# One ring of three shared PSUM pairs for attention scores, and x transposed by DMA

## The chip, the core and the metric

One core of one Trainium2 chip. The metric is the device time in us of one execution, taken on the chip; lower is better. Profiles are single executions; their span (first to last instruction) is some 1.8 us shorter than the same execution's device time. The kernel before takes 811.6 us (median; 811.2 to 812.7).

The names used below: PE is the matmul engine; ACT (ScalarE) and DVE (VectorE) work on vectors; SP serves here to issue transfers (DMA), and ACT's queue issues some too. PE writes its results to banks of PSUM, and two banks make a "pair". A "pass" is the scores of two heads in one pair, a "fill" is PE writing a pass, a "visit" is a run of fills with no other PE work between. PV is the product of the exponentiated scores with V; mish is the activation of branch B. The "head" of the span lasts until the first exp, the "tail" begins when the last exp has ended, and the "stretch" lies between.

## The reference

Input x is 2048 x 640 (bf16). Two branches read it, and a gate mixes them:

```python
g = sigmoid((x * gate_w).sum(-1, keepdims=True))
# A: 32 heads of 20 columns, full softmax attention over 2048 keys, then wo (640 x 640)
scores = einsum("bhqd,bhkd->bhqk", q, k) * 20 ** -0.5
a = (softmax(scores) @ v) @ wo
# B: dense 640 -> 1536, mish, dense 1536 -> 640
h = x @ w1 + b1
b = (h * tanh(softplus(h))) @ w2
out = g * a + (1 - g) * b
```

The exps of the scores are the bulk of the work: 32 heads x 2048 x 2048.

## The kernel before

The kernel does not run in the order of its text. Every piece of work is a task with an engine, an estimated cost and its needs; a planner (`Order.run`) walks through a model of the engines at build time and emits the tasks in the order in which the model starts them. The order on each engine is therefore fixed before the launch, and any change of a cost, a need or a constant may give a wholly different order.

Heads are taken in groups `G` of four heads by 512 queries (32 groups). For each group and each of 16 blocks of 128 keys, the scores of four heads are made in two passes, each with two PE matmuls into a pair of PSUM banks. Most key blocks are exponentiated by ACT (one ACTIVATE of 128x1024 for a pass). `SHARE[G]` of the 16 blocks go to DVE, which builds a bit-level approximation in three terms (per block two L779 for the first, a half each, and two L793 for the others). A "PV" matmul group then adds the result to the output of the head.

```python
SHARE = (3, 3, 4, 5, 4, 6, ...)          # key blocks for DVE by group, 143 in all
...
R = {k: Ring(...) for k, n in (
    ("S0", 1), ("S1", 1), ("X", 1), ("D", 1), ("E", (13, 6, 48)), ...)}   # PSUM: S0, S1, D pairs; X, C single banks
...
ld_x = {0: [load_x((nc.scalar, nc.sync)[s % 2], s, s + 1, ...) for s in range(4)]}
ld_w0 = [load((nc.sync, nc.scalar)[t], w0[:, t], ...) for t in range(2)]   # weights of the first four heads
ld_x[1] = [load_x(nc.sync, 4, 8, 6500)]
ld_wv = load(nc.sync, wv, ...)
ld_x[2] = [load_x(nc.scalar, 8, 12, 9000)]
ld_x[3] = [load_x(nc.sync, 12, 16, 11000)]
ld_gw = load(nc.sync, gw[:, :, 0:1], ...)
ld_wqk = load(nc.sync, wqk[:, :, 0:2 * D], ...)
...
for s in range(4):                        # chunk 0 of x: PE transposes, then a copy; tile 1 by ACT
    ...
    (nc.scalar.copy if s == 1 else nc.vector.tensor_copy)(out=xt[:, 0, :, s * P:(s + 1) * P], ...)
for c in range(1, 4):                     # chunks 1 to 3: PE transposes, copies by DVE
    ...
for n, blk in enumerate(passes):          # passes for ACT: two buffers by turns
    sb, eb = Buf(R["S%d" % (n % 2)]), Buf(R["E"])
    ...
    nc.scalar.activation(eb.tile[:, 0:w * QC], sb.tile[:, 0:w * QC], ACT.Exp, scale=inv)
...
xb = Buf(R["D"])                          # passes for DVE: a buffer of their own
```

The softmax here doesn't subtract the row's maximum and nothing guards it: scores larger than these inputs give would overflow.

## Time and profile before

| | before |
|---|---|
| device time, median | 811.6 us |
| first exp starts | 10.3 us |
| stretch from the first exp to the end of the last | 781.6 us, 738 exps |
| tail after it | 19.3 us |

Which lines carry this, and how they are read, is in the prediction. Two more views of the kernel before are needed later. First, what the queues waited for (engine and line, what it waited for, us, times, longest; a q behind an engine's name is its sequencer, which also issues DMAs):

```profile
SPq L423 <- DVE xt L472: 1.6, 1, 1.6
SPq L423 <- DMA arena<-in_A_x_dram: 1.2, 1, 1.2
```

L423 is the line that issues a load. An issue that waits for an earlier transfer to land (the second line: wv's issue at 3.83 us waited for an x tile that landed at 3.81) is a thing to note. Second, the chain of waits up to the first exp (start, length, what):

```profile
1.65 7.26 DMA wvt<-in_A_wqkv_dram
...
8.95 0.46 PE S L557 x20
9.42 0.49 PE D L557 x12
9.90 0.42 PE S L716 x4
10.33 1.92 ACT es L744 x2
```

The first exp hangs on the landing of the first weights at 8.9 us; ACT's own queue does not appear after 1.6 us.

### The profile page before, as it was taken

The numbers are of one execution on the slowest core, as the hardware profiler recorded it, in microseconds if no ns is written. First come the engines' busy times: TensorE is split into PE (matmuls) and PEld (weight loads), VectorE is DVE, ScalarE is ACT, GpSimd is POOL, SyncE is SP. The second block draws the span as 40 slices with busy tenths as digits, with TensorE's granted clock in tenths as the row PEclk, the third lists the DMA queues.
The fourth block names the chain that finished last, engine by engine and source line by source line (L and its number), as shares of the span: only waits on it lengthen the run. The fifth ranks groups of instructions, "written<-read, shape, count | busy, mean of one in ns | idle before, by whom it ended". The sixth has DMA issues, their size and how long they took to land.

```text
span 811.1 us, 24412 instructions
## 1 busy us (share of the span) xinstructions
PE 776.3 (96%) x10642; PEld 281.7 (35%) x10642; DVE 706.3 (87%) x949; ACT 774.0 (95%) x791; POOL 6.6 (1%) x10
## 2 busy tenths in 40 slices
PE   8999999999999989999999998999999989999998
PEld 4432333333333333333332334333332333333336
DVE  3788899998888899999999998889999989978994
ACT  5899999999999999999999999999999999999991
POOL 3000000000000000000000000000000000000000
PEclk9999999999999999999999999999999999999999
DMA  9601100000000000000000000000000000001112
GB/s 314 186 16 24 19 16 7 19 19 16 18 8 19 19 15 6 19 20 20 20 19 15 22 4 19 16 19 19 20 7 19 19 19 4 20 19 32 32 40 76
DMA packets 32273, 25.21 MB, mean 31 GB/s; under 512 B 17762, under 2 KB 26914, under 8 KB 32166
## 3 DMA queue, kind: packets, MB, share of 16 engines
q1 hardware_dynamic: 30694, 22.55, 9.9%
q8 instruction: 83, 1.36, 0.7%
q10 hardware_dynamic: 1472, 1.10, 0.4%
q14 instruction: 24, 0.20, 0.1%
HBM read 18.20 MB, written 2.88 MB: 26 GB/s over the span
## 4 chain that ended last, share of the span: by engine, by line
PE 58%; ACT 33%; DVE 4%; issue 4%; DMA 1%; ACTq 0%; DVEq 0%
ACT es L744 23%; PE S L716 19%; PE C L703 17%; PE X L517 11%; ACT arena L933 7%; PE X L577 3%; PE X L557 3%; DVE t L779 2%; PE X L597 1%; ACT bs L744 1%; PE D L517 1%; DMA wvt<-in_A_wqkv_dram 1%; PE D L716 1%; ACT L933 1%; PE C L399 1%
## 5 line engine op out<-in xcount | busy, mean ns | idle before, releaser
L744 ACT ACTIVATE es<-S 128x1024 bf16<-128x1024 f32 x708 | 666.5, 1033 | 13.2 <-PE C L703 4.6
L779 DVE TENSOR_SCALAR t<-D 128x1024 uint16<-128x1024 f32 x286 | 349.2, 1221 | 52.1 <-PE D L716 48.5
L716 PE MATMUL S<-q,kt 32*128 32x512 bf16 x1476 | 285.9, 384 | 15.7 <-ACT es L744 12.1
L793 DVE TENSOR_SCALAR t<-t 128x2048 uint16<-128x2048 uint16 x286 | 190.2, 681 | 1.3
L716 PEld LDWEIGHTS <-kt 32*128 32x128 bf16 x2048 | 80.5, 91 | 273.7 <-issue 263.5
L703 PE MATMUL C<-es,va 128*32 128x512 bf16 x1416 | 140.6, 385 | 1.3 <-DVE oraw L826 1.2
L716 PE MATMUL D<-q,kt 32*128 32x512 bf16 x572 | 111.3, 385 | 4.1 <-DVE t L779 3.5
L703 PE MATMUL C<-t,vs 128*32 128x512 bf16 x1144 | 106.3, 383 | 0.3 <-DVE t L793 0.2
L517 PE MATMUL X<-w,arena 128*32 128x320 bf16 x1536 | 82.0, 305 | 0.1
L703 PEld LDWEIGHTS <-va 128*32 128x32 bf16 x2048 | 54.5, 95 | 79.3 <-issue 65.1
L517 PE MATMUL X<-xt,w 128*32 128x512 bf16 x960 | 72.3, 383 | 2.5 <-DVE arena L919 1.4
L933 ACT ACTIVATE arena<-arena 128x2048 bf16<-128x2048 bf16 x36 | 68.0, 1911 | 0.3
L703 PE MATMUL C<-t,va 128*32 128x512 bf16 x572 | 58.0, 383 | 1.7 <-DVE t L779 1.7
L517 PEld LDWEIGHTS <-arena 128*32 128x32 bf16 x1536 | 33.4, 96 | 33.5 <-issue 26.4
L557 PE MATMUL X<-xt,wqk 128*32 128x512 bf16 x560 | 44.2, 383 | 0.0
L577 PE MATMUL X<-xt,wqk 128*32 128x512 bf16 x560 | 43.8, 383 | 0.0
L919 DVE TENSOR_SCALAR arena<-X,b 128x512 bf16<-128x512 f32 x48 | 35.7, 745 | 4.8 <-PE X L517 4.5
L703 PEld LDWEIGHTS <-vs 128*32 128x32 bf16 x1144 | 29.9, 95 | 28.3 <-issue 20.5
L517 PEld LDWEIGHTS <-w 128*32 128x32 bf16 x960 | 22.7, 95 | 30.6 <-issue 22.7
L744 ACT ACTIVATE bs<-S 128x1024 bf16<-128x1024 f32 x30 | 29.7, 1031 | 0.8 <-PE S L716 0.6
L597 PE MATMUL X<-wvt,xt 128*128 128x160 bf16 x310 | 28.3, 234 | 1.9 <-DVE va L602 0.9
L399 PE MATMUL C<-xt,gw 128*32 128x512 bf16 (+4 forms) x396 | 28.1, 359 | 0.0
(92 smaller groups left out, 362.0 us busy)
## 6 DMA issues: line engine op xcount, KB each, us to landing
rbc<-rows SPq DMA_DIRECT2D x124, 64.0 KB
w<-in_B_w_dram SPq DMA_DIRECT2D x2, 1920.0 KB
out_dram<-arena SPq DMA_DIRECT2D x16, 160.0 KB
oc<-on SPq DMA_DIRECT2D x96, 20.0 KB
wqk<-in_A_wqkv_dram SPq DMA_DIRECT2D x1, 1600.0 KB
arena<-in_A_x_dram SPq DMA_DIRECT2D x2, 640.0 KB
wvt<-in_A_wqkv_dram SPq DMA_DIRECT2D x1, 800.0 KB
arena<-in_A_x_dram ACTq DMA_DIRECT2D x1, 640.0 KB
```

The lines of the kernel that those rows point to most:

```text
L399: nc.tensor.matmul(t[32 * r:32 * r + 32, 0:n], lhsT=gw[:, 0, 1:33], rhs=xt[:, r, 0, 0:n], start=G is None, stop=G is None, tile_position=( ...
L517: nc.tensor.matmul(t[32 * r:32 * r + 32, 0:width], lhsT=lhsT(r), rhs=rhs, start=a, stop=b, tile_position=(0, 32 * r))
L557: nc.tensor.matmul(t[32 * r:32 * r + 32, 0:n], lhsT=w, rhs=xt[:, sc, k, lo:hi], start=k == 0, stop=k == KT - 1, tile_position=(0, 32 * r))
L577: nc.tensor.matmul(t[32 * r:32 * r + 32, 0:QC], lhsT=w, rhs=xt[:, qc, k, :], start=k == 0, stop=k == KT - 1, tile_position=(0, 32 * r))
L597: nc.tensor.matmul(t[:, n * 160:(n + 1) * 160], lhsT=xt[:, js[n] // 4, k, (js[n] % 4) * P:(js[n] % 4 + 1) * P], rhs=wv[:, k, 160 * b:160 * ...
L703: nc.tensor.matmul(acc[G][32 * r:32 * r + 32, :], lhsT=vs4[:, b, term - 1, DVE_KEYS.index(j), h:h + 32] if term else va4[:, b, j, h:h + 32 ...
L716: nc.tensor.matmul(t[:, off * QC:(off + 1) * QC], lhsT=kt[32 * r:32 * r + 32, (p % 2) * S + j * P:(p % 2) * S + (j + 1) * P], rhs=q_buf[G] ...
L744: nc.scalar.activation(eb.tile[:, 0:w * QC], sb.tile[:, 0:w * QC], ACT.Exp, scale=inv)
L779: nc.vector.tensor_scalar(out=bufs[0].tile[:, 2 * QC * hp:2 * QC * (hp + 1)], in0=xb.tile, scalar1=P * LOG2E * inv, scalar2=P * (127 - log ...
L793: (nc.vector if eng == "DVE" else nc.gpsimd).tensor_scalar(out=bufs[i].tile[:, a * w:(a + 1) * w], in0=bufs[0].tile[:, a * w:(a + 1) * w], ...
L919: lambda t: nc.vector.tensor_scalar(out=hs[:, ft, :], in0=t[:, 0:QC], scalar1=b1[:, ft:ft + 1], scalar2=None, op0=ALU.add),
L933: nc.scalar.activation(v, hs[:, 4 * a:4 * a + 4, :] if i == 0 else v, func, bias=1.0 if i == 1 else 0.0)
```

## The change

Its intent: any of three pairs serves ACT or DVE, so that a score pass need not wait for its own fixed buffer; two ACT passes may be filled in one visit of PE where two pairs are free; the planner's latencies are corrected; chunks 1 to 3 of x are transposed on their way in by DMA, which frees PE and DVE at the start; and all constants are searched anew for the planner. The core of the diff (cut: the other constants, the planner's latencies, single-line cost changes, the deterministic order of the last four small steps):

```diff
-SHARE = (3, 3, 4, 5, 4, 6, ...)      # 143 key blocks to DVE
+SHARE = (2, 3, 4, 5, 5, 5, ...)      # 133
...
-        ("S0", 1), ("S1", 1), ("X", 1), ("D", 1), ("E", (13, 6, 48)), ...
+        ("S", 3), ("X", 1), ("E", (17, 6, 56)), ...
...
-        sb, eb = Buf(R["S%d" % (n % 2)]), Buf(R["E"])
+        sb, eb = Buf(R["S"]), Buf(R["E"])
...
-            xb = Buf(R["D"])
+            xb = Buf(R["S"])
...
+        if S and S[1].before2:           # pick_pe: wait for two free pairs, or until it is late for one
+            ...
+                free = S[1].rings[0].ring.free
+                if len(free) > 1:
+                    end = free[1][0]
+                last = 0 if self.mode == "row" else (S[1].before.end or ...) - self.EARLY
+                S = max(S[0], min(end + self.LAT["ACT"], last)), S[1]
...
-    ld_x = {0: [...]}; ld_w0 = [load((nc.sync, nc.scalar)[t], ...)]; ld_x[1] ... ld_wv, ld_gw, ld_wqk by nc.sync
+    ld_x = [load((nc.scalar, nc.sync)[t % 2], xs[:, t, :], ...) for t in range(NU)]     # chunk 0 alone
+    for c in range(1, NQ):
+        for k in range(KT):
+            t_xt[c, k] = o.add("SP", 5000, lambda c=c, k=k: nc.sync.dma_start_transpose(
+                out=xt[:, c, k, :], in_=x2d[c * QC:(c + 1) * QC, k * P:(k + 1) * P]), prio=0)
+    ld_w0 = [load(nc.scalar, w0[:, t], ...) for t in range(2)]
+    ld_wv = load(nc.scalar, wv, ...)
+    ld_gw = load(nc.scalar, gw[:, :, 0:1], ...)
+    ld_wqk = load(nc.scalar, wqk[:, :, 0:2 * D], ...)
...
-    for c in range(1, 4):                # PE transposes and DVE copies of chunks 1 to 3
-        ...
```

## The prediction

> **What bounds the kernel now.** I first read the page's share of busy time and the 40 slices, then the groups of instructions, then one table by stage, and last the start times of the exps one by one.
>
> ```profile
> PE 776.3 (96%) x10642; PEld 281.7 (35%) x10642; DVE 706.3 (87%) x949; ACT 774.0 (95%) x791; POOL 6.6 (1%) x10
> ...
> L744 ACT ACTIVATE es<-S 128x1024 bf16<-128x1024 f32 x708 | 666.5, 1033 | 13.2 <-PE C L703 4.6
> L779 DVE TENSOR_SCALAR t<-D 128x1024 uint16<-128x1024 f32 x286 | 349.2, 1221 | 52.1 <-PE D L716 48.5
> L716 PE MATMUL S<-q,kt 32*128 32x512 bf16 x1476 | 285.9, 384 | 15.7 <-ACT es L744 12.1
> L793 DVE TENSOR_SCALAR t<-t 128x2048 uint16<-128x2048 uint16 x286 | 190.2, 681 | 1.3
> ...
> L399 PE MATMUL C<-xt,gw 128*32 128x512 bf16 (+4 forms) x396 | 28.1, 359 | 0.0
> ```
>
> PE and ACT are both near full, but PE's share contains 28.1 us of matmuls that only keep its clock up (L399), so PE has some room. ACT has none: its work is 738 exps (708 to es, 30 to bs) and 36 mish passes. The stage table says where ACT is not busy (columns: stretch, its length, PE, PEld, DVE, ACT, POOL, clock, DMA share, GB/s):
>
> ```profile
> 0.00:10.30 10.30, 7.48 (x90) 3.65 (x94) 2.54 (x13) 2.56 (x3) 6.11 (x8) 1.00 0.82 251
> 10.30:50.00 39.70, 36.36 (x440) 16.42 (x438) 28.39 (x52) 35.23 (x38) 0.00 (x0) 1.00 0.58 191
> 50.00:400.00 350.00, 338.32 (x4504) 117.51 (x4500) 312.85 (x417) 346.84 (x354) 0.51 (x2) 1.00 0.07 17
> 400.00:791.90 391.90, 378.81 (x5228) 132.38 (x5223) 353.55 (x456) 386.56 (x394) 0.00 (x0) 1.00 0.07 19
> 791.90:811.00 19.10, 15.32 (x400) 11.77 (x393) 8.96 (x13) 2.77 (x5) 0.00 (x0) 0.96 0.23 80
> ```
>
> So the span is a head of 10.3 us (until the first exp), an ACT stretch of 781.6, and a tail of 19.2. In the stretch ACT looks idle for only 13 us. That hides most of the loss, because exps overlap: one lasts 1.03 us, but in the timeline the next can start 0.90 after it.
>
> ```profile
> 67.62 1.02 ACT L744 ACTIVATE bs<-S 128x1024 bf16<-128x1024 f32 x1
> 68.52 1.03 ACT L744 ACTIVATE es<-S 128x1024 bf16<-128x1024 f32 x1
> 69.42 1.05 ACT L744 ACTIVATE bs<-S 128x1024 bf16<-128x1024 f32 x1
> ```
>
> I took the start-to-start time of all 723 exps that follow an exp: 349 at about 904 ns, 181 at about 920, and a long tail up to 4.4 us. Together 689.8 us, mean 954. 723 x 0.904 = 653.6, so 36.2 us are lost to late scores, not 13. The other 91.8 us of the stretch (781.6 - 689.8) are mish, table loads and steps into and out of them. Setting each exp beside its fill gives the cause: in the groups that come late by under 0.4 us, the exp starts 486 ns after its last score matmul, and that matmul came late because PE was in other work when the pair became free. One example:
>
> ```profile
> 351.39 0.40 PE L703 MATMUL C<-t,vs 128*32 128x512 bf16 x4
> 351.54 1.22 DVE L779 TENSOR_SCALAR t<-D 128x1024 uint16<-128x1024 f32 x1 [0.75 <-PE D L716]
> 351.62 0.72 PE L517 MATMUL X<-w,arena 128*32 128x320 bf16 x16
> 352.27 0.39 PE L716 MATMUL S<-q,kt 32*128 32x512 bf16 x2
> 352.59 0.32 PE L517 MATMUL X<-w,arena 128*32 128x320 bf16 x4
> 352.76 1.94 ACT L744 ACTIVATE es<-S 128x1024 bf16<-128x1024 f32 x2 [0.18 <-PE S L716]
> ```
>
> The exp at 352.76 follows its fill (352.27) by 0.49; sixteen dense matmuls stood ahead of it. The idle column says 0.18, the start-to-start loss is 0.30. With two pairs (S0, S1) a fill must start within some 0.29 us of the end of the exp two before it (1.81 - 1.03 - 0.49), and one PE group with its switch uses that up.
>
> **What the Trainium skill says.** "ScalarE: Activation LUTs", What ACT_TABLE_LOAD costs: an ACTIVATE with immediates takes 186 ns + 0.833 N (1039 for N = 1024) and back-to-back ones overlap by about 93 ns. The trace agrees on the length (1033) and shows a larger overlap, about 0.13. "TensorEngine Tiling (Array Packing)", Key Properties: changing the tiling mode drains PE. The trace agrees: a score pass comes 312 ns after the last column group and the next column group 318 after it, where two column groups stand 216 apart; a visit thus costs 318 + 312 - 216 = 414 ns net, and a visit with two pairs (325) 421. "Perfetto Trace Analysis", Identifying the Most-Contended Engine: repeating gaps on the engine that should be full can mean too few PSUM buffers; that is the pattern here. "DMA: Bandwidth & Descriptors", DMA Transpose (X-bar): bf16 may be transposed on its way into SBUF, from SP or ACT alone; the kernel before has no such transfer, so no trace confirms its speed yet.
>
> **The change part by part.** *Shares.* The DVE list sums to 133 keys in place of 143. A key is two exps on ACT or two L779 and two L793 on DVE. ACT gets 20 more exps (758): 20 x 0.904 = +18.1 us, wholly on the bound. DVE loses 20 x (1.221 + 0.681) = 38.0. PE loses 20 PV groups of 0.216 (three terms become one), 4.3 us.
>
> *Ring.* S0, S1 and D become three pairs that any score pass may take. Passes stay 1024 in all (738 + 286 before, 758 + 266 after). Before, 735 visits held them, 275 of them with two. If the scheduler now gets some 620 visits, PE saves 115 x 0.41 = 47 us, which is slack for being on time, not time off the end. The size of the gain is the part of the 36.2 us that goes. By class: the 181 at 920 ns (2.9 us) stay, since their fills are not late. The 185 between 930 and 1300 (26.2 us) are the late fills; I keep a quarter, 6.5. A single fill into a third free pair would have 0.9 us more room; but two S pairs filled in one visit come when only one full pair is left, so their slack is again about 0.29 us, and DVE still holds a pair for the 1.22 us of L779. Hence a quarter and not zero. The 7 above 1300 (7.4 us) include 3.5 us at 30.6 where ACT waited for a PV (exp buffers full); the exp ring grows from 13 to 17 slots, so I keep 3.0. Sum left: 12.4.
>
> *DMA transposes.* Gone are 60 PE transposes (4.7 us at an estimated 78 ns, from eight in 0.62) and nine evictions (6 x 0.69 + 3 x 0.42 = 5.4 us of DVE), all beside exps in the first 31 us. New are 15 transfers of 128 KB on SP. In the head, DMA is 82% busy, and the first K product waited 0.84 us for its weights. Those weights now move to ACT's queue ahead of wv, which should help; but all remaining weight loads are issued from ACT before its first copy. On SP the last two of them, gw and wqk, took 1.97 and 2.51 us to issue; on ACT they would hold up the copy that Q needs. I net this at +0.5, between -1 and +4. Tail: the pairs of the last product rotate over three buffers, but PE is busy for 15.3 of 19.1 us there, so -0.5.
>
> Sum of the span: head 10.3 + exps (723 + 20) x 0.904 = 671.7 + other ACT 91.8 + tail 19.2 = 793.0 with no stall at all; + 12.4 stalls + 0.5 - 0.5 = 805.4. The timed runs lie 0.4 over the traced span: 805.8, say 805.5.
>
> **Rivals.** (a) The stalls vanish. DVE falls to 706.3 - 38.0 - 5.4 = 663 and PE gains room, so nothing else binds; time 794 to 797. For it: 26 of the 36 us are one mechanism, aimed at directly. Against: orders are fixed beforehand, and a paired fill is as tight as before. (b) The ring moves the wait: an L779 fill takes the pair that the next exp needs. Then the 36 us stay and the 20 exps come on top: 793.0 + 36 = 829. Against: pairs in use are about 758 x 1.5 + 266 x 1.75 = 1603 of 3 x 780 us, 68%. (c) The head turns into the loss: ACT's queue blocked, or slow transposes starving K of keys 4 to 15, for 3 to 10 us: 808 to 816. For it: DMA is 58% busy even from 10 to 50 us. Against: key 4 is not needed until eight exps are done, near 17.6 us.
>
> **Range and chances.** A 2% gain needs 795.3, that is, stalls of about 2 us in place of 36; only (a) in full, or a shorter head or tail with it, gives that: 0.13. A 2% loss needs 827.8, (b) in full: 0.05. The rest, 0.82, is in between. Range 796 (nearly (a)) to 816 ((c), or half the stalls kept).
>
> **What would show it.** Right: 758 exps; their mean start-to-start near 0.92 (0.904 + 12.4/743); more than two thirds at or under 0.92; under 650 visits; DVE near 663 us; first exp within 11 us; tail near 19. Wrong: a mean still near 0.95; ACT's waits naming L779 through the score tile; the first exp past 13 us, or gaps before 35 us ended by a DMA.

## The result

The changed kernel takes 818.4 us (median of 4; 817.7 to 820.5) against 811.6: ratio 1.0086, 95% interval 1.0065 to 1.0106. A ratio is not quite the ratio of the medians. So the change costs 0.9%, clear of noise but within 2%. The result lies above the predicted range (796 to 816).

The page of the kernel after, the lines that answer to those of before (L758 is the exp, L793 and L807 the DVE pair, L729 the score matmul):

```profile
PE 773.8 (95%) x10406; PEld 283.6 (35%) x10406; DVE 664.5 (81%) x900; ACT 778.3 (95%) x811; POOL 6.6 (1%) x10
...
L758 ACT ACTIVATE es<-S 128x1024 bf16<-128x1024 f32 x714 | 661.1, 1163 | 6.3 <-PE S L729 5.1
L793 DVE TENSOR_SCALAR t<-S 128x1024 uint16<-128x1024 f32 x266 | 324.3, 1219 | 66.0 <-PE S L729 65.0
L729 PE MATMUL S<-q,kt 32*128 32x512 bf16 x2048 | 296.4, 382 | 16.0 <-ACT es L758 9.8
```

ACT's largest group of exps lasts longer in the mean (1163 ns against 1033), although they follow each other faster: their scores are there earlier, so more of each exp overlaps with the one before. Again the start-to-start times tell more than the durations. The stages of the kernel after, cut at its first exp and at the end of its last (columns as in the prediction):

```profile
0.00:20.70 20.70, 10.06 (x94) 4.74 (x94) 3.10 (x14) 2.56 (x3) 6.12 (x8) 0.76 1.00 222
20.70:50.00 29.30, 26.91 (x310) 12.06 (x306) 15.49 (x31) 28.03 (x31) 0.00 (x0) 1.00 0.73 189
50.00:400.00 350.00, 337.67 (x4425) 118.16 (x4427) 303.48 (x410) 348.21 (x361) 0.00 (x0) 1.00 0.07 17
400.00:798.50 398.50, 385.51 (x5229) 138.13 (x5222) 333.98 (x436) 396.68 (x413) 0.52 (x2) 1.00 0.07 19
798.50:815.90 17.40, 13.68 (x364) 10.48 (x357) 8.50 (x12) 2.83 (x6) 0.00 (x0) 1.00 0.23 78
```

The first row is the news: the head has doubled, from 10.3 to 20.8 us, with ACT busy for 2.6 of it and DMA full (share 1.00). Its chain of waits:

```profile
2.05 3.85 DMA arena<-in_A_x_dram
...
5.92 7.34 DMA wvt<-in_A_wqkv_dram
...
13.28 0.38 ACTq L453
...
13.70 1.28 ACT L505
14.99 0.70 ACT xt L505
15.73 2.32 PE S L590 x15
18.05 2.13 PE S L570 x30
20.19 0.60 PE S L729 x4
20.79 5.58 ACT es L758 x6
```

Read from below: exps, first scores, K (L570), Q (L590), then ACT's copy of the second x tile at 14.99 with the table load before it (13.70), and before those an issue by ACT's sequencer at 13.28 (L453, the load of wqk), which came as soon as the transfer of wv had landed at 13.26. All weight loads stand on ACT's queue ahead of the copy. In the trace's records, the issue of wqk waits for the very completion semaphore that wv was given: eight of them are handed out in turn over both queues, and an issue that gets a used one waits for its former transfer. ACT's queue so issued wv at 5.92, when an x tile had landed (5.90), gw at 8.80, when a transposed piece had (8.72), and wqk at 13.28, and the copy had to stand behind them. The issues themselves are short, as two lines of the timeline show; the time lies in the waits before them. The view of waits names the last:

```profile
8.80 0.43 ACTq L453 DMA_DIRECT2D gw<-in_gate_w_dram  x1
13.28 0.38 ACTq L453 DMA_DIRECT2D wqk<-in_A_wqkv_dram  x1
...
ACT L505 <- DMA wvt<-in_A_wqkv_dram: 13.7, 1, 13.7
```

The planner could not see this: it books the issues of ACT's queue on an engine of its own, "AQ", at 0.45 us each, apart from ACT. Replayed off the chip, its model has the first exp at 9.8 us in the kernel after, and at 9.2 in that before.

DMA is full throughout the head, and the transposes take more of it than the plain loads that they replace. The page's line of packets, before and after:

```profile
DMA packets 32273, 25.21 MB, mean 31 GB/s; under 512 B 17762, under 2 KB 26914, under 8 KB 32166
```

```profile
DMA packets 38847, 25.18 MB, mean 31 GB/s; under 512 B 25874, under 2 KB 33490, under 8 KB 38742
```

The same bytes move in some 6,600 more packets. In the records the 15 transposes are 7,680 packets of 256 B, 24 ns each in the mean: 7680 x 0.024 = 184 us of engine time. Loaded plainly, the same three chunks were 1,536 packets of 1,280 B at about 62 ns, 95 us. Packets of different transfers overlap, so a packet's time contains what else moves: where transposes ran nearly alone (the version j_late_wqk below, 18 to 23 us), a packet of 256 B took 18 ns, which would make 138 us. So a transposed byte took 1.5 to 2 times the engine time of a plain one.

Start-to-start times of the exps, read from the records as in the prediction ("lost" is the sum over 904 ns each; "late" are those 930 to 1300 ns after the one before, "large" those over 1300):

| | head | stretch | exps | mean | lost | late: number, us | large: number, us | tail | span |
|---|---|---|---|---|---|---|---|---|---|
| before | 10.3 | 781.6 | 738 | 954 ns | 36.2 | 185, 26.2 | 7, 7.4 | 19.3 | 811.1 |
| after | 20.8 | 777.8 | 758 | 922 ns | 13.3 | 53, 5.7 | 6, 5.4 | 17.3 | 815.9 |

So 20 more exps (+18 us) and 23 us fewer lost make the stretch 4 us shorter, the tail is 2 us shorter, and the head 10.5 us longer.

### The profile page after: what moved, and what is told of

Its sections match the earlier page's. It is cut to its first block, busy times and chain, and to the rows that moved or that the text cites. A ratio compares the mean times of both kernels' runs of the same rounds, so it can differ in the third digit from the quotient of the medians.

```text
span 815.9 us, 23922 instructions
## 1 busy us (share of the span) xinstructions
PE 773.8 (95%) x10406; PEld 283.6 (35%) x10406; DVE 664.5 (81%) x900; ACT 778.3 (95%) x811; POOL 6.6 (1%) x10
## 4 chain that ended last, share of the span: by engine, by line
PE 49%; ACT 36%; DVE 5%; issue 5%; DMA 4%; SPq 1%; ACTq 0%; DVEq 0%
ACT es L758 26%; PE S L729 17%; PE C L716 14%; PE X L530 9%; ACT arena L947 6%; PE X L590 3%; DVE t L793 3%; PE X L570 2%; PE S L530 2%; ACT bs L758 2%; DMA rbc<-rows 1%; DMA wvt<-in_A_wqkv_dram 1%; DVE t L807 1%; ACT oc L758 1%; DMA rows<-rec 1%
## 5 line engine op out<-in xcount | busy, mean ns | idle before, releaser
L758 ACT ACTIVATE es<-S 128x1024 bf16<-128x1024 f32 x714 | 661.1, 1163 | 6.3 <-PE S L729 5.1
L793 DVE TENSOR_SCALAR t<-S 128x1024 uint16<-128x1024 f32 x266 | 324.3, 1219 | 66.0 <-PE S L729 65.0
L729 PE MATMUL S<-q,kt 32*128 32x512 bf16 x2048 | 296.4, 382 | 16.0 <-ACT es L758 9.8
L729 PEld LDWEIGHTS <-kt 32*128 32x128 bf16 x2048 | 96.1, 91 | 284.6 <-issue 276.8
L807 DVE TENSOR_SCALAR t<-t 128x2048 uint16<-128x2048 uint16 x266 | 174.4, 683 | 2.1
L716 PE MATMUL C<-t,vs 128*32 128x512 bf16 x1064 | 98.8, 382 | 0.7 <-DVE t L807 0.6
L716 PEld LDWEIGHTS <-va 128*32 128x32 bf16 x2048 | 50.8, 95 | 73.9 <-issue 64.7
L716 PE MATMUL C<-t,va 128*32 128x512 bf16 x532 | 54.7, 384 | 1.4 <-DVE oraw L840 0.8
L570 PE MATMUL X<-xt,wqk 128*32 128x512 bf16 x560 | 44.4, 383 | 0.1
L590 PE MATMUL X<-xt,wqk 128*32 128x512 bf16 x560 | 44.0, 383 | 0.3 <-DVE kt L574 0.3
L716 PEld LDWEIGHTS <-vs 128*32 128x32 bf16 x1064 | 29.1, 95 | 24.7 <-issue 18.2
L758 ACT ACTIVATE bs<-S 128x1024 bf16<-128x1024 f32 x28 | 27.7, 1154 | 0.0
L598 DVE CAST q<-X 128x512 bf16<-128x512 f32 x31 | 21.2, 683 | 7.8 <-PE X L590 7.6
L610 PEld LDWEIGHTS <-xt 128*128 128x128 bf16 x320 | 22.2, 97 | 15.3 <-issue 14.9
```

Of the source, the lines that this page charges most:

```text
L570: nc.tensor.matmul(t[32 * r:32 * r + 32, 0:n], lhsT=w, rhs=xt[:, sc, k, lo:hi], start=k == 0, stop=k == KT - 1, tile_position=(0, 32 * r))
L590: nc.tensor.matmul(t[32 * r:32 * r + 32, 0:QC], lhsT=w, rhs=xt[:, qc, k, :], start=k == 0, stop=k == KT - 1, tile_position=(0, 32 * r))
L598: nc.vector.tensor_copy(out=buf.tile, in_=t[:, 0:QC])
L610: nc.tensor.matmul(t[:, n * 160:(n + 1) * 160], lhsT=xt[:, js[n] // 4, k, (js[n] % 4) * P:(js[n] % 4 + 1) * P], rhs=wv[:, k, 160 * b:160 * ...
L716: nc.tensor.matmul(acc[G][32 * r:32 * r + 32, :], lhsT=vs4[:, b, term - 1, DVE_KEYS.index(j), h:h + 32] if term else va4[:, b, j, h:h + 32 ...
L729: nc.tensor.matmul(t[:, off * QC:(off + 1) * QC], lhsT=kt[32 * r:32 * r + 32, (p % 2) * S + j * P:(p % 2) * S + (j + 1) * P], rhs=q_buf[G] ...
```

## The experiments

The table gives all twelve; texts follow. The span is that of the profiled run, the time the median of four runs, the ratio that to the kernel before. The first four ran on one chip (before: 813.4 us there), c2, j, f and k on a second (811.8), m, n, q and r on a third (813.1), so kernels are compared by the ratio.

Read one more number beside the table: the mean granted PE clock of each run. In every kernel here the slowest of its runs has the lowest clock, or shares it. Of j_late_wqk, the profiled run took 814.3 us at 0.989, the other three 809.1 to 811.3 at 0.998. So a profile may show a loss that most runs of the same kernel don't have.

| | head | stretch | exps | late | large | tail | span | time | ratio (95%) |
|---|---|---|---|---|---|---|---|---|---|
| a_pe_x | 11.0 | 800.2 | 758 | 44, 4.0 | 16, 25.2 | 17.4 | 828.5 | 830.3 | 1.0209 (1.0171-1.0247) |
| b_dma_x_only | 20.2 | 785.1 | 738 | 168, 24.9 | 14, 12.5 | 20.1 | 825.4 | 827.9 | 1.0156 (1.0104-1.0208) |
| c_act_free | 14.9 | 791.3 | 758 | 48, 5.1 | 7, 15.5 | 17.4 | 823.6 | 827.0 | 1.0172 (1.0107-1.0236) |
| d_w_on_sp | 11.1 | 787.4 | 758 | 51, 5.5 | 13, 14.9 | 17.4 | 815.8 | 817.7 | 1.0044 (1.0004-1.0084) |
| c2_act_free_same_plan | 15.7 | 779.8 | 758 | 54, 5.8 | 10, 7.3 | 17.4 | 812.8 | 814.1 | 1.0028 (1.0004-1.0053) |
| j_late_wqk | 11.6 | 783.6 | 758 | 52, 6.0 | 13, 11.0 | 17.3 | 812.5 | 810.7 | 0.9979 (0.9962-0.9995) |
| f_old_ring | 10.4 | 797.9 | 758 | 96, 14.2 | 20, 18.4 | 17.9 | 826.2 | 827.2 | 1.0190 (1.0167-1.0213) |
| k_late_share | 11.3 | 802.7 | 738 | 39, 4.1 | 19, 45.3 | 23.5 | 837.4 | 836.4 | 1.0298 (1.0263-1.0333) |
| m_single | 21.2 | 816.0 | 758 | 36, 4.4 | 23, 43.8 | 17.3 | 854.4 | 852.9 | 1.0507 (1.0483-1.0530) |
| n_late_warm | 13.2 | 779.2 | 758 | 50, 5.6 | 7, 6.8 | 17.3 | 809.7 | 811.1 | 0.9986 (0.9963-1.0009) |
| q_late_tuned | 11.4 | 780.4 | 760 | 52, 6.1 | 5, 6.2 | 17.4 | 809.2 | 813.6 | 1.0025 (0.9985-1.0065) |
| r_pex_tuned | 10.3 | 791.1 | 760 | 48, 5.3 | 13, 16.0 | 17.4 | 818.7 | 819.6 | 1.0089 (1.0066-1.0112) |

### a_pe_x: the x part undone

```diff
-    ld_x = [load(... chunk 0 ...)]; t_xt[c, k] = ... nc.sync.dma_start_transpose(...); weights by nc.scalar
+    # loads of all of x over both queues, weights, PE transposes and DVE copies as in the kernel before,
+    # with pairs from the new ring: buf = Buf(R["XS"[(c + i) % 2]])
```

> The new kernel with its x part undone: all 16 x tiles loaded plainly over both queues as before, chunks 1 to 3 transposed on PE and copied by DVE, weights loaded as before; the ring, the fill rule and all constants stay new. Theory H (the whole loss is the head: first exp at 20.8 us in place of 10.3): first exp near 10.3 us, ACT stretch and tail as in the new kernel (777.8 and 17.4 us), span near 805.5, time near 807, some 1.3% under the new kernel and 0.5% under the kernel before. Rival R (the ring profits from the PE and DVE time that the DMA transposes freed): the stretch grows again by 5 us or more, time 812 or over.

Measured: the head fell to 11.0 us as expected, but the stretch grew by 22 us. The time is 830.3. The late fills stayed gone (44 exps, 4.0 us); what came are 16 large gaps with 25.2 us, and 9 us more around mish. Neither theory had this: the rival foresaw a longer stretch, but from lost PE time, and late fills did not return. The planner had made a new order for which the constants were never searched; its own model, replayed, books the end of the last exp 22 us later than for the kernel after (798.9 against 776.9) at the same first exp, and the stretch grew by as much. A kernel of this kind can't be taken apart by an edit that makes it plan anew, unless one reads the parts (head, late, large) and not the time.

### b_dma_x_only: the x part alone, in the kernel before

```diff
+    # loads, transposes by DMA and weights on ACT's queue as in the new kernel; rings and constants of before
```

> The kernel before with the new x part alone (DMA transposes, all weight loads on ACT's queue); old rings, old constants, and the order of the last four small steps fixed as in the new kernel. Theory H: first exp near 20.8 us, about 10.5 us later than before, and the time near 822. Rival: if the later start is partly caught up because the old stretch lost several us in its first 50 us (exp buffers full at 30 us), the time is 816 to 819.

Measured: first exp at 20.2 us, 9.9 later than before, with the old rings; the late fills are those of the old rings (168, 24.9 us). So the head belongs to the x part and the late fills do not. The time is 5.9 us above the 822 of theory H, and not below it as in the rival; but the kernel before took 813.4 on this chip, and by the ratio the time is 824 where the kernel before takes 811.6. The stretch grew by 3.5 us (new order) and the tail by 0.8. The four runs spread from 821.4, at a mean clock of 0.996, to 828.5, at 0.986.

### c_act_free and c2_act_free_same_plan: ACT out of the path of the head

```diff
-            (nc.scalar.copy if s == 1 else nc.vector.tensor_copy)(
+            nc.vector.tensor_copy(
...
-                nc.scalar.copy(out=buf.tile, in_=t[:, 0:QC])      # first q
+                nc.vector.tensor_copy(out=buf.tile, in_=t[:, 0:QC])
+    # c alone: the planner books both on DVE too, so it makes a new order; c2: emitted only, the order stays
```

> The new kernel, with ACT's two small jobs in the head (the copy of the second x tile, the cast of the first q) given to DVE; every DMA stays where it is. Theory Q (ACT's queue is blocked by its own DMA issues until 13.7 us, and the copy behind them holds up the first Q product): Q starts near 8.5 us, and the first exp is now held only by ACT's table load, which ends near 15.0 us; time about 5.8 us less, near 812.6. Rival D (the transposes crowd the DMA engines and the x tiles and weights arrive late anyway): first exp still at 19 us or later, time 817 or over.

> As c_act_free, but the planner is told nothing: it still books both jobs on ACT, so the order on every engine stays that of the new kernel, and only the two instructions are emitted on DVE. Theory P (in c_act_free a new order, not the head, ate the gain: its exp stretch was 791 us against 778): first exp again at 14.9 us, stretch 778 to 780, span 810 to 811.5, time 812 to 813.3. Rival D (late transposes and weights starve the start anyway): the stretch grows by what the head gains, span 814 or over.

Measured: in c_act_free Q started at 8.39 us and the first exp at 14.89, both as theory Q had it; every transfer was where it had been, so it was the copy behind the issues and not the x data that held Q until 15.7. Its time nevertheless rose (827.0), from the new order: large gaps 15.5 us, among them one wait of 5.2 for a PV group, and 9 us more around mish. With the order kept (c2) the first exp came at 15.7 us, somewhat later than in c; stretch 779.8; span 812.8 against 815.9; time 814.1. That is theory P, with a gain 1 us smaller than stated, in part from the later start.

### d_w_on_sp: wv, gw and wqk issued from SP, among the transposes

```diff
-    ld_wv = load(nc.scalar, ...); ld_gw = load(nc.scalar, ...); ld_wqk = load(nc.scalar, ...)
+    ld_wv = load(nc.sync, ...);   ld_gw = load(nc.sync, ...);   ld_wqk = load(nc.sync, ...)
```

> The new kernel, with the loads of wv, gw and wqk issued from SP, among the transposes, in place of ACT. ACT then issues only two x tiles and the two parts of w0. Theory Q: ACT is free by about 3 us, the copy is done by 7, the first exp comes at 12 to 13 us (the last x tile lands 2 us later than in the kernel before), time 809.5 to 811. Rival D: the first exp stays past 18 us. A further risk under either: the transposes now wait behind wv, and K of keys 4 to 7 comes late, seen as gaps of ACT between 15 and 30 us.

Measured: same order on the engines; first exp at 11.07 us, 9.7 earlier, even a little better than theory Q said. But the time was 817.7 (ratio 1.0044, where the kernel after has 1.0086; the intervals overlap), since the named further risk came about in full:

```profile
17.72 0.32 PE L610 MATMUL X<-wvt,xt 128*128 128x160 bf16 x1 [5.22 <-DMA xt<-in_A_x_dram]
...
20.07 1.02 ACT L758 ACTIVATE es<-S 128x1024 bf16<-128x1024 f32 x1 [6.15 <-PE S L729]
```

These are two lines of the timeline of this run. PE stands still for 5.2 us for a transposed piece of chunk 1, and ACT for 6.2 us for the scores behind it. By the completion semaphores the last two pieces of chunk 1 landed at 17.7 and 18.2 us; in the kernel after all five had landed by 13.8. wqk (1.6 MB), which landed at 17.2, now ran ahead of them on the same queue. PE's clock was at half from 13.7 to 30.8 us. The head's 10 us had become 9.7 us more loss in the first 50 us (11.4 against 1.7).

### j_late_wqk: gw and wqk issued from SP behind the last transpose

```diff
-    ld_gw = load(nc.scalar, gw[:, :, 0:1], ...)
-    ld_wqk = load(nc.scalar, wqk[:, :, 0:2 * D], ...)
+    # both issued by nc.sync right after the transpose (c, k) == (NQ - 1, KT - 1); the planner's booking is kept
```

> The new kernel in its own order; gw and wqk (1.6 MB, first used some 70 us later) are issued from SP behind the last transpose in place of from ACT. wv stays on ACT. Both causes of the head should go at once: ACT is free at about 6 us, and wqk no longer runs ahead of the transposes of chunk 1, which in d_w_on_sp landed at 17.7 to 18.6 us and in the new kernel by 13.8. First exp at 11 to 11.5 us, gaps of ACT before 25 us under 2.5 us together, span 807 to 809.5, time 809 to 811. If the transposes still starve K of key 4 (gap over 4 us near 15 us), crowding by the transposes alone is enough, and the span stays over 811.

Measured: 810.7 us, ratio 0.9979 to the kernel before, with an interval just under 1: by the ratios it beats the kernel after by some 1%, and is the one version whose interval lies below the kernel before, by 0.2%. That is little for the best of twelve versions, tested by four runs. The first exp came at 11.55 us. Of the 9.2 us gained there, 5.6 were given back in the first 50 us (loss 7.3 against 1.7), more than the 2.5 that I had allowed. That is the loss of the profiled run, with a span of 812.5 us; the other three spanned 807.3 to 809.5, at the higher clock. The piece of chunk 1 that the chain names landed at 14.1 us. Where the given-back time went is shown in the next experiment's windows.

### n_late_warm: six useless matmuls where PE waits

```diff
         def mm(t, n):
+            if b == 0 and js[0] == 2 and n == 0:
+                for _ in range(6):
+                    nc.tensor.matmul(t[:, 0:QC], lhsT=kt[:, 0:P], rhs=kt[:, 0:QC], start=True, stop=True)
```

> j_late_wqk in the same order, with 6 matmuls of 512 columns of no use put ahead of the second V unit, where PE waits 1.2 us for wv with a clock that then falls to half until 26 us. Theory cold (of the 7.3 us that j_late_wqk loses in its first 50 us, some 4 come from score fills at half clock): granted clock 1.0 from 14 to 26 us, the loss in the first 50 us falls to 4 or less, time 806 to 808. Rival (the fills wait for K of chunk 1 by DMA, not for the clock): clock 1.0, loss still 6 to 8 us, time 810 to 811. Or the clock stays at half, as PE waits for data anyway: no change.

The same two windows of j_late_wqk, of n_late_warm and of the kernel before (the third column from the right is the granted clock):

```profile
14.00:20.00 6.00, 5.76 (x36) 1.54 (x37) 1.25 (x2) 3.52 (x5) 0.00 (x0) 0.50 1.00 123
20.00:26.00 6.00, 5.96 (x44) 3.10 (x47) 1.96 (x8) 5.20 (x6) 0.00 (x0) 0.50 0.46 83
```

```profile
14.00:20.00 6.00, 4.97 (x52) 2.44 (x50) 1.57 (x4) 6.00 (x8) 0.00 (x0) 1.00 0.80 105
20.00:26.00 6.00, 5.41 (x68) 2.27 (x67) 3.52 (x8) 6.00 (x7) 0.00 (x0) 1.00 0.53 111
```

```profile
14.00:20.00 6.00, 5.59 (x70) 2.79 (x71) 3.08 (x6) 5.54 (x7) 0.00 (x0) 1.00 1.03 395
20.00:26.00 6.00, 5.39 (x71) 2.01 (x69) 3.56 (x6) 5.54 (x7) 0.00 (x0) 1.00 0.94 284
```

In j_late_wqk (first fence) PE is busy for 96% and 99% of these 12 us and yet gets through 36 and 44 matmuls, against 70 and 71 in the kernel before (last fence): at a granted clock of 0.50, which lasted from 14.0 to 27.6 us, each matmul takes about twice as long. In n_late_warm (second fence) the clock is whole in these windows, ACT is busy in all of them (6.00), and the loss in the first 50 us fell from 7.3 to 3.2 us (1.7 in the kernel after). So theory cold can account for some 4 of the 5.6 us given back. It is not alone: in this profiled run another half-clock phase, from 9.0 to 12.4 us, moved the first exp from 11.55 to 13.15, and exps that start 1.6 us later may wait less for the pieces of chunk 1. The two are not told apart. The time is 811.1, not 806 to 808, and the recorded clocks say why the matmuls gained nothing there: half the clock for 13.6 of 812 us takes 0.008 off the mean, so the three runs of j_late_wqk at 0.998 can't have had the phase that the matmuls were to prevent, and all four runs here lie at 0.997 or 0.998 as well.

### q_late_tuned: j_late_wqk, with the constants searched for its own landings

```diff
-SHARE = (2, 3, 4, 5, 5, 5, ...);  DENSE = (1.15, 7.85, 13.7, 18.45)   # and MISH, DOWN, OUT
+SHARE = (2, 3, 4, 5, 4, 5, ...);  DENSE = (-0.05, 7.85, 13.7, 18.45)
-    t_xt[c, k] = o.add("SP", 5000, ...);  t_xt[c, k].issue = 1270;  ld_wv = load(nc.scalar, wv, ..., 8000)
+    t_xt[c, k] = o.add("SP", 6500, ...);  t_xt[c, k].issue = 1350;  ld_wv = load(nc.scalar, wv, ..., 10800)
```

> j_late_wqk with the planner told when the transfers really land (wv 10.8 us after its issue, a transpose 6.5 us after its issue and one issue in 1.35 us), and the constants searched again with the planner alone (760 exps). The planner now expects an end 2.8 us later than for the new kernel. Theory (the start of the new kernel was planned with transfers that come too early): gaps in the first 50 us shrink from 7.3 to under 4 us, time 806 to 810. Rival (a new order costs more than the better start gives, as in a_pe_x and c_act_free): time 815 or over.

Measured: the loss in the first 50 us fell to 2.5 us, as expected of an order that knows when the pieces land; first exp at 11.4, and the profiled run has the shortest span of all, 809.2. Two of its four runs took 811 us and two 816 to 817, so the ratio, 1.0025 with an interval of 0.9985 to 1.0065, is not to be told from 1. It is no better version than j_late_wqk. The two pairs differ in the mean granted clock: 0.997 and 0.998 in the faster, 0.990 and 0.992 in the slower. What lowered it is open, since only a faster one was profiled.

### r_pex_tuned: a_pe_x, with the constants searched for it

```diff
-DENSE = (1.15, 7.85, 13.7, 18.45); MISH = (2.2, 3.7, 3.8, 4.15); DOWN = (2.35, -0.9, 6.35, 7.25); ...
+DENSE = (1.15, 6.35, 13.7, 18.45); MISH = (2.2, 4.6, 2.1, 4.15); DOWN = (3.4, -1.05, 7.05, 3.65); ...   # SHARE, KEYS, VALUES, OUT too
```

> a_pe_x (PE transposes) with its constants searched again with the planner alone, which books the end 9.8 us earlier than for a_pe_x (760 exps). Theory (a_pe_x lost to the new kernel by its untuned order alone, which showed in exps over 1300 ns: 25.2 us): those fall under 16 us, first exp at 11 us, time 818 to 822. Rival: the large waits come from the PE transposes themselves; they stay over 20 us, time near 830.

Measured: 819.6 us against 830.3 of a_pe_x; the large gaps fell from 25.2 to 16.0 us. The two kernels differ in nothing but the order and its shares, so order alone is worth some 10 us here (10.7 by the times, 1.2% by the ratios). That confirms what a_pe_x suggested: its 830 said little about PE transposes. Its stretch is still 13 us longer than that of the kernel after. Whether a longer search would close this, or whether PE transposes cost it, stays open.

### f_old_ring: the old ring, with everything else of a_pe_x

```diff
-        ("S", 3), ("X", 1), ("E", (17, 6, 56)), ...
+        ("S0", 1), ("S1", 1), ("X", 1), ("D", 1), ("E", (17, 6, 56)), ...
-        sb, eb = Buf(R["S"]), Buf(R["E"])
+        sb, eb = Buf(R["S%d" % (n % 2)]), Buf(R["E"])
-        ps, ts.before, ts.before2 = ts, prev, marks[n - 2] if n > 1 else None
+        ps, ts.before, ts.before2 = ts, prev, None      # without the new wait for free pairs
-            xb = Buf(R["S"])
+            xb = Buf(R["D"])
```

> As a_pe_x (new constants, PE transposes), but with the old rings S0, S1, D and the old rule for a fill; latencies, exp ring of 17 and shares stay new. Theory ring (the third shared pair and the paired fill remove the late fills): the class of exps 930 to 1300 ns after the one before rises from 44 (4.0 us lost) in a_pe_x to 150 or more, over 20 us lost, as in the kernel before (185, 26.2 us) and b_dma_x_only (168, 24.9). Rival (the planner's corrected latencies and switch costs did it): the class stays under 70 and 8 us. The time is not the measure here, as every new order brings its own few large stalls; it should be over 835 under theory ring, as ACT keeps 758 exps.

Measured: 96 late exps with 14.2 us, between the two theories and meeting neither. The kernel before has 26.2, this one 14.2, a_pe_x 4.0. This one and the kernel before share the score rings and do without the wait for free pairs, but differ in the planner's latencies and other small rules, the constants (shares among them) and the size of the exp ring; so these together took 12 us of the late fills, and the ring of scores with its rule the other 10, as far as one order of each can tell. PE's visits to scores were 735, 769 and 697 in the same order. The time is 827.2, a little less than a_pe_x's 830.3 (ratios 1.0190 and 1.0209, not told apart), where more than 835 was expected: the 10 us that the ring takes from the late fills a_pe_x lost elsewhere, 6.8 of them in large gaps (25.2 against 18.4).

### k_late_share: j_late_wqk with the old shares

```diff
-SHARE = (2, 3, 4, 5, 5, 5, ...)      # 133
+SHARE = (3, 3, 4, 5, 4, 6, ...)      # 143, as before
```

> As j_late_wqk, with the old list of DVE shares (143 keys, 738 exps in place of 758). A new order comes with it. Theory share (20 exps cost 18.1 us of the bound, and the ring does not need the lower share): the class 930 to 1300 stays under 80 exps and 9 us; exps back to back 653.6 us plus stalls; stretch 760 plus the large stalls of a new, untuned order (13 to 22 us in a_pe_x and c_act_free), so 773 to 785, span 802 to 814. Rival (DVE at 143 keys now holds the shared pairs too long): the class 930 to 1300 over 120 exps, and ACT's waits name L793.

Measured: 738 exps, and late fills still gone (39, 4.1 us). So their going does not need DVE's lower share, and that rival falls. But the order was not searched for these shares, and ACT stood still for PV groups (L721), which in this kernel means that no exp buffer was free:

```profile
ACT es L763 <- PE C L721: 34.7, 10, 9.2
```

Ten waits, 34.7 us. The 18 us that 20 fewer exps save are more than lost: stretch 802.7, tail 23.5, time 836.4. Whether a searched order could keep 143 keys on DVE and the new ring stays open.

### m_single: the third pair, filled one pass at a time

```diff
-                S = max(S[0], min(end + self.LAT["ACT"], last)), S[1]
+                pass
...
-            if S and S[0] <= now + self.BESIDE and not set(S[1].rows) & self.rows:
+            if S and self.pe[-1].prio == 1 and S[0] <= now + self.BESIDE and not set(S[1].rows) & self.rows:
```

> The new kernel without the paired fill of two exp passes: a pass is filled as soon as a pair is free, two in a visit only if one of them is for DVE. Three shared pairs stay; x by DMA stays; the order is new. Theory of the prediction (a single fill into a third pair has 0.9 us more room, so pairing is what keeps late fills): late class (930 to 1300 ns) under 25 exps and 3 us, against 53 and 5.7 in the new kernel; visits of PE to scores rise from 696 to over 780. Rival (pairing is what relieves PE, and without it fills come late): late class over 100 exps and 12 us. The first exp stays at 20.8 us; the time, with an untuned order, over 820.

Measured: late exps 36 with 4.4 us, in the class of the late fills as good as the kernel after, and visits of PE to scores 722 and not over 780. But the edit took away only a third of what it was to remove: replayed off the chip, the planner's order has two or more ACT passes in 41 of these 722 visits, in 64 of 696 in the kernel after and in 22 of 735 in that before. With fewer such visits the late fills did not return, so the result points to the third pair as such and not to the filling of two in one visit; a version with no such visit was not run. Neither theory's figures were met. The rest is again an order that nobody searched: large gaps 43.8 us (27.6 us of waits for PV), stretch 816.0, time 852.9.

## Why the prediction was wrong

By its own sum of the span, 805.4, beside the profiled run after, 815.9:

| step | predicted | measured |
|---|---|---|
| exps | 758 | 758 |
| mean start-to-start | 0.92 us | 0.922 |
| stalls: late, 920 class, large | 6.5 + 2.9 + 3.0 = 12.4 us | 5.7 + 2.2 + 5.4 = 13.3 |
| stretch | 775.9 us (671.7 + 91.8 + 12.4) | 777.8 |
| DVE busy | 663 us | 664.5 |
| visits of PE to scores | 620, under 650 | 696 |
| head | 10.3 + 0.5 = 10.8 us | 20.8 |
| tail | 19.2 - 0.5 = 18.7 us | 17.3 |
| timed runs over the span | 0.4 us | 1.8 |

(Fills counted as late in the table are all those between 930 and 1300 ns, as in the prediction.) The differences add up: 805.4 + 10.0 (head) + 1.9 (stretch) - 1.4 (tail) = 815.9.

**The step that failed is the head: "I net this at +0.5, between -1 and +4".** It measured +10.5. The prediction named the right operations: all weight loads issued from ACT before its first copy, with gw and wqk "1.97 and 2.51 us to issue". It took those durations for the price. On ACT the two issues took 0.43 and 0.38 us; the price was the wait ahead of each issue for an earlier transfer to land, 3.1 us before wv, 2.5 before gw and 4.0 before wqk, until wv had landed at 13.26. The kernel before had shown such a wait, in the line that has wv's issue wait 1.2 us for an x load; I had not asked what the same issues would wait for on ACT. (The 1.97 and 2.51 us were something else: the transfers that had had the semaphores of gw and wqk landed at 4.87 and 4.53 us there, before those issues began at 5.13 and 7.15. Why they were long stays open.) Rival (c) named the blocked queue and put the time at 808 to 816, at a size of 3 to 10 us; it was held to be the less likely one, and it came, a bit beyond its end.

How the 10.5 us divide: with gw and wqk off ACT's queue (d_w_on_sp, j_late_wqk) the first exp comes at 11.07 and 11.55, so 9.2 to 9.7 us are the blocked queue. What is left over, 0.8 to 1.2 us, fits the later x: PE's last transposes of chunk 0 start at 7.42 us in the kernel after, when their tile has landed, and at 5.61 in that before. This last attribution is argued, not tested. Of the 9.2 us of j_late_wqk, 6.9 are the wait itself (Q starts at 8.84 us in place of 15.73), and 2.3 are PE at half clock after it: the clock was at 0.50 from 10.7 to 20.9 us in the kernel after, Q took 2.32 us against 1.26 in j_late_wqk, and from the start of Q to the first exp it was 5.1 us against 2.7.

**The head's loss is not all there is to gain.** Freed, the head gave 9.2 to 9.7 us, and in the profiled runs the first 50 us took 9.7 (d_w_on_sp) or 5.6 us (j_late_wqk) back, by transposed pieces that landed late and by a PE at half clock. That the transposes take 1.5 to 2 times the DMA time of plain loads is measured; that this is the reason why the change gains nothing over PE transposes is not shown, since neither version with PE transposes had an order searched as fully.

**The other steps held.** The late fills went as said, to 5.7 us, and they stay at 4.0 to 6.1 us in all eleven kernels with the new ring. The cause given, the ring, is half the cause: about 12 us came from the planner's latencies, the constants and the exp ring (f_old_ring against before; not split further), and about 10 from the ring (a_pe_x against f_old_ring). The saving of visits was put too high (696 came, 620 were expected; the order is fixed before the launch, so they could have been counted) and did not matter: m_single has 722 visits and as few late fills. The large gaps came out at 5.4 in place of 3.0, none of them of weight. The last row of the table is a slip: I took the profiled span of one run from the median of other runs; the profiled run of the kernel before itself took 813.0 us for its span of 811.1. It would have made the prediction 1.4 us higher. Two more slips change nothing: 98% of 811.6 is 795.4, not 795.3, and the passage of "Perfetto Trace Analysis" on repeating gaps stands under Optimization Strategy; the prediction named another section.

What stays open: whether fewer exps on ACT (143 keys on DVE) would pay with the new ring and a searched order; what PE transposes would do with one; and what sets off a half-clock phase in one run and not in the next of the same kernel, by which runs spread over 5 us. The best version found is j_late_wqk: ratio to the kernel before 0.9979 (0.9962 to 0.9995).

## What to carry to other kernels

An engine whose first piece of work is on the path should not issue loads ahead of it: an issue can wait for an earlier transfer to land, and all that stands behind it on the queue waits too (here 9.2 to 9.7 us), so look at the gaps before the issues and not only at their lengths, and at whether the planner's model has the issues on the right engine. Where the order is planned at build time, an edit that makes a new order moves the time by 10 to 20 us for no reason of its own: keep the order, or judge by parts (head, late fills, large gaps) and not by the time. And where instructions overlap, read start-to-start times: the idle column showed 13 us where 36 were lost. Before explaining a profile, compare its clock with that of the kernel's other runs.

## What the Trainium skill lacked or had wrong

- "Advanced Engine Details and Errata", X-Bar Transpose (TRN2), says that transposing DMAs are as fast as regular ones. Here the 15 transposes moved in packets of 256 B at 24 ns each, 184 us of engine time, against about 95 us for the same bytes loaded plainly in packets of 1,280 B at about 62 ns; at the 18 ns of the stretch where they ran nearly alone it would be 138 us. Each also took 1.1 to 2.5 us to issue (median 1.26 in j_late_wqk), which the section does not mention: with 128 KB in each, j_late_wqk moved 105 GB/s from 18 to 23 us at a DMA share of 0.50.
- "TensorE: Matmul & The Clock Gate", What's actually happening, gives about 3.4 us of sustained activity for the return to full clock. In the profiled run of j_late_wqk the granted clock stayed at 0.50 from 14.0 to 27.6 us while PE was busy for 96% of the time from 14 to 20 us and 99% of that from 20 to 26. What the section's activity monitor counts as idle there, no run shows.
- On no page did I find that a DMA issue waits for an earlier transfer when completion semaphores are handed out in turn, and that the issuing engine's queue stands meanwhile. Here it held ACT until 13.3 us.
